# A fused attention and mixture-of-experts kernel: the row maxima travel another way, and four operands are laid out anew

## The chip, the cores and the metric

The kernel runs on one core of a Trainium2 chip. The metric is the device time of one execution, in microseconds. The core has a tensor engine (PE, with its weight loads shown apart as PEld), a vector engine (DVE), a scalar engine (ACT), a general engine (POOL) and a queue engine (SP) that here only issues transfers. Sixteen DMA engines move data between HBM and SBUF for all of them.

## The reference, cut to what matters

```python
B, H, S, D = 4, 8, 576, 64
scores = q @ k.T / 8 ; scores[above the diagonal] = -1e9
a = exp(scores - scores.max(-1)) ; a /= a.sum(-1) + 1e-9
local = a @ v
q_p = where(q > 0, q, exp(q) - 1) + 1
mem_out = (q_p @ M_prev) / (q_p . z_prev + 1e-6)
x = sigmoid(beta) * mem_out + (1 - sigmoid(beta)) * local      # [B*S=2304, 512]
# eight experts of 288 tokens each, filled greedily by the order of all logits x @ w_gate
x[mask] = maximum(x[mask] @ w1[e], 0) @ w2[e]
out = maximum(maximum(x @ w1, x @ w2), x @ w3) @ w_out
```

## The kernel before, in words

The program has three stages: attention (32 heads as 16 pairs, four pairs per batch), routing (a search for each expert's threshold), and the experts with the final block. The change touches the first stage only.

For each pair SP loads K and Q transposed (`Kr`, `Qr`, 128 partitions: the same 64 rows are loaded twice, once into each half), Q in another layout (`QN`), the memory matrix (`MZ`), and V (`V`, `VT`). The two copies serve a split of fp32 into a rounded part and a rest: `KX` holds rounded K above its rest, `QX` rounded Q twice, `KB`/`QL` the rounded K and the rest of Q.

A head's scores are computed twice. First as `s` (line 480, and 482 for the last 64 rows of both heads together), from which DVE takes minus the row maximum over 8 into a column of `nm` (line 499, one column per block of 128 rows, nine columns per pair). Then transposed as `t` (lines 598 and 599); the second product there has a 65th row of `QL` that carries the row maximum, so that ACT can take `exp` straight from PSUM (line 609) into `PT`. POOL zeroes the triangle above the diagonal (line 627), PE multiplies by V (`av`, line 642), DVE normalizes (lines 660 to 671) and adds onto `x`, into which the memory part (`mem`, line 691) was written before (line 710). Eight further columns of `x` carry the routing logits.

The row maxima stand in `nm` as columns over 128 partitions, and are wanted as one row on partition 64 of `QL`. For pairs 1 to 15 DVE copies them (`nmr`, line 533), SP writes them transposed to HBM (`nmd`, line 536, one element of 4 bytes at a time), waits, and reads them back as rows (lines 543 and 544, twice for each head). Pair 0 uses small products with an identity instead (line 559).

Beside this the stage converts the weights of the final block from 64 to 32 bits (`conv`, lines 817 to 837: a load `m2raw`, then ACT and DVE); after each batch SP stores `x` to HBM (`xd`, line 801).

The order of all this is not that of the code. `Plan.run` simulates the engines with costs and latencies that are written beside each task (`add(key, {engine: ns}, fn, deps, new, use)`), and the tasks are then emitted in the order of their simulated start; each engine and each queue runs its part strictly in that order. `new` takes a buffer out of a ring (`BUFS` has their sizes) and `use` holds it. A transfer on SP is planned as a cost on SP plus a latency (2000, or `NLAT` = 3000 for the row maxima). `fill` products without a use (line 749) keep PE occupied while the first loads come.

Of the kernel before, what the change touches and what calls it, by code (L numbers as in the profile page):

```python
# [22 lines left out]
F32 = mybir.dt.float32  # L23
# [10 lines left out]
NJ = 5  # L34
# [6 lines left out]
FILL = (48, 256)  # L41
# [13 lines left out]
BUFS = {'Kr': 2, 'Qr': 2, 'QN': 2, 'MZ': 2, 'V': 3, 'VT': 2, 'phi': 2, 'ph': 1, 'KX': 6, 'QX': 5, 'QL': 3, 'KB': 6, 'QJ': 4, 'nm': 3, 'nmr': 4, 'PT': 2, 's': 3, 't': 2, 'r5': 2, 'tmp': 3, 'rm': 2, 'x': 2, 'm2raw': 1, 'm2a': 1, 'm2b': 1}  # L55
# [172 lines left out]
def attention(g, tc, ctx, consts, beta, qT, kT, qN, v1, vT, mz, mT, wg, xd, nmd, L, m2):  # L228
# [12 lines left out]
    warm = mask[:, :256].bitcast(BF)  # L241
# [79 lines left out]
    pairs, xs, stores = [], {}, {}  # L321
    W = PRIO

    def pair(p):
# [3 lines left out]
        b_ = {n: Buf(R[n]) for n in ("Kr", "Qr", "QN", "MZ", "V", "VT", "phi", "ph")}  # L328
# [46 lines left out]
        tM = add(k0 + .2, {"SP": 300}, ldmz, new=[b_["MZ"]])  # L375
# [46 lines left out]
        def head(i):  # L422
            bh = {x: Buf(R[x]) for x in ("KX", "QX", "QL", "KB")}
            r.bh[i] = bh
            kh = n + 5 * i + W["prep"]

            def ck(e):
                r.KX[i] = tile("KX", [128, S], F32R)
                copy(e, r.KX[i], r.Kr[:, i])

            def cq(e):
                r.QX[i] = tile("QX", [128, S], F32R)
                copy(e, r.QX[i], r.Qr[:, i])
# [18 lines left out]
            t3 = add(kh + .1, sb, sk, [t1], use=[b_["Kr"], bh["KX"]])  # L452
            t4 = add(kh + .1, sb, sq, [t2], new=[bh["QL"]], use=[b_["Qr"], bh["QX"]])
# [8 lines left out]
    def maxes(r, p):  # L462
# [110 lines left out]
    def unit(r, p, i):  # L573
# [14 lines left out]
        for gi, gr in enumerate(groups):  # L588
# [22 lines left out]
            t = add(n1 + W["T"] + .1 * gi, {"PE": (430, 590, 460, 80)[gi]}, fT, r.th[i] + r.tb[i] + [tN] + (fill if h == 1 and gi == 3 else []),  # L611
# [22 lines left out]
        for j in range(NJ):  # L634
            m = rows(j)

            def fA(e, j=j, m=m):
                av = av3(AV[h % 2])
                for kb in range(j + 1):
# [6 lines left out]
                           mk[:1] + (fill if h == 1 else []) + (ex[1:2] if j else []) + (mk[1:2] if j > 1 else []) + (mk[2:] if j > 3 else []) + [r.tV],  # L646
# [3 lines left out]
    def norm(r, p, i, deps, mems):  # L650
# [25 lines left out]
        c = {"POOL": 920, "DVE": dve(360)}  # L676
        return add(n + .3, {x: c[x] for x in (W["xadd"] if p < NP - 1 else ("POOL", "DVE"))}, f4, [t] + mems, use=[bt, r.bx])

    def mem(r, p, part):
# [36 lines left out]
        return add(n + .3, {"DVE": dve(144 * k)}, f3, [t] + ([firsts[b]] if b in firsts else []),  # L716
                   new=[pend[b]] if first else [], use=[bm, br] + ([] if first else [pend[b]]))
# [3 lines left out]
    def gate(r, b, h0, h1, deps):  # L721
# [57 lines left out]
    for p in range(NP):  # L779
# [14 lines left out]
        if pp == H // 2 - 1:  # L794
            gate(r, b, H - 2 if b == B - 1 else 0, H, stores[b])

            def st(e, b=b):
                x = xs[b]
# [4 lines left out]
            add(r.n + 9 + W["gate"], {"SP": 6000}, st, stores[b], use=[r.bx])  # L803
# [652 lines left out]
def program(tc, qT, kT, qN, v1, vT, mz, mT, beta, wg, wr, w1, w2, w3, wo, out):  # L1456
    g = K()
    g.rounds, g.elist = [], []
    with tc.manual_schedule(), ExitStack() as top:
# [3 lines left out]
        nmd = dr.tile([B * H // 2, 9, 128], F32, name="nmd")  # L1463
# [5 lines left out]
        with ExitStack() as ctx:  # L1469
            attention(g, tc, ctx, consts, beta, qT, kT, qN, v1, vT, mz, mT, wg, xd, nmd, L, (w1, w2, w3, wo))  # L1470
# [8 lines left out]
def layout(i):  # L1479
    import numpy as np  # L1480
    d = {}
    for n in "qk":
        d[n + "T"] = np.ascontiguousarray(i[n].reshape(B, H // 2, 2, S, D).transpose(0, 1, 4, 2, 3))
# [12 lines left out]
    d["mz"] = mz  # L1496
# [26 lines left out]
```

## Time and profile before

| | us |
|---|---|
| median of 3 runs (1086.93 to 1127.53) | 1096.24 |
| the profiled execution's own time | 1086.32 |
| its span, first to last instruction | 1084.5 |

| engine | busy us | share of the span |
|---|---|---|
| PE | 944.3 | 87% |
| DVE | 598.3 | 55% |
| POOL | 366.2 | 34% |
| ACT | 312.3 | 29% |

The profile shows for each stretch of time how long each engine was busy, which of its two levels of clock TensorE was granted (1.00 is 2.4 GHz, 0.50 is 1.2 GHz, values between are means over a stretch), and the busy share of the 16 DMA engines with what they moved. A matmul that runs at the lower clock counts as busy for longer, so a busy PE isn't a PE at its best. A wait is put down to what ended last before it.

### The profile page before, as it was taken

How to read it: one execution, taken by the hardware profiler on the slowest of the kernel's cores; microseconds unless marked ns; L12 is line 12 of the kernel's file. 1: busy time of each engine (PE TensorE's matmuls, PEld its weight loads, DVE VectorE, ACT ScalarE, POOL GpSimd, SP SyncE). 2: the span in 40 equal slices, each digit the busy share in tenths (PEclk: the TensorE clock that was granted, in tenths of full speed). 3: DMA queues.
4: the chain of work that ended last, by engine and by line, in shares of the span. 5: the costliest groups of instructions: out<-in, count | busy, mean ns of one | idle time of the engine just before them, and what ended most of it. 6: DMA issues, size and time to landing. Idle time of an engine off the chain costs nothing.

```text
span 1084.5 us, 17202 instructions
## 1 busy us (share of the span) xinstructions
PE 944.3 (87%) x6494; PEld 869.0 (80%) x6494; DVE 598.3 (55%) x1664; ACT 312.3 (29%) x675; POOL 366.2 (34%) x344
## 2 busy tenths in 40 slices
PE   8697979987798993489799899899899799879997
PEld 6576868876687882489699799798799698779996
DVE  8556755575668548755627637538337447513221
ACT  5223321232334223041231332222331322332311
POOL 4233422342345128130630631522521523450301
PEclk8657855575859586589999899999899899899999
DMA  8777765869667711240610511602501602451100
GB/s 231 144 104 114 127 175 74 137 111 158 124 148 179 95 23 44 51 127 15 122 62 18 122 60 40 138 21 61 127 21 57 122 21 59 125 133 39 40 1 30
DMA packets 73338, 97.59 MB, mean 90 GB/s; under 512 B 46218, under 2 KB 48266, under 8 KB 73256
## 3 DMA queue, kind: packets, MB, share of 16 engines
q1 hardware_dynamic: 70280, 87.06, 40.0%
q0 software_dynamic: 2976, 9.44, 2.6%
q8 instruction: 51, 0.84, 0.3%
q14 instruction: 31, 0.25, 0.1%
HBM read 86.97 MB, written 9.52 MB: 89 GB/s over the span
## 4 chain that ended last, share of the span: by engine, by line
PE 54%; DMA 22%; DVE 12%; issue 7%; POOL 2%; ACT 1%; SPq 1%; POOLq 0%; DVEq 0%; ACTq 0%
PE av L642 7%; PE w L1270 7%; PE w L1272 7%; PE w L1271 7%; DMA m2raw<-in_m2w 6%; PE acc L1270 4%; DMA wraw<-in_wr 4%; PE acc L1272 4%; PE acc L1271 4%; DMA xg<-xd,tidx 3%; PE t L598 2%; PE s L480 2%; PE t L599 2%; DMA MZ<-in_mz 2%; DMA Qr<-in_qT 2%
## 5 line engine op out<-in xcount | busy, mean ns | idle before, releaser
L1240 POOL TENSOR_TENSOR wlo<-wraw,whi 128x1024 fp32r<-128x1024 f32 x57 | 139.3, 2448 | 308.3 <-ACT whi L1236 308.1
L1270 PE MATMUL w<-yh,mh 128*128 128x288 f32 x576 | 174.9, 304 | 8.4 <-ACT mt L1372 5.7
L1271 PE MATMUL w<-yl,mh 128*128 128x288 f32 x576 | 172.2, 299 | 0.0
L1272 PE MATMUL w<-yh,ml 128*128 128x288 f32 x576 | 171.6, 298 | 0.0
L642 PEld LDWEIGHTS av<-V,PT 128*128 128x128 f32 (+2 forms) x960 | 148.5, 230 | 14.6 <-issue 4.8
L642 PE MATMUL av<-V,PT 128*128 128x73 f32 (+2 forms) x960 | 157.4, 319 | 0.0
L1270 PEld LDWEIGHTS w<-yh,mh 128*128 128x128 f32 x576 | 110.4, 192 | 12.8 <-ACT mt L1372 5.9
L1271 PEld LDWEIGHTS w<-yl,mh 128*128 128x128 f32 x576 | 110.5, 192 | 3.5
L1272 PEld LDWEIGHTS w<-yh,ml 128*128 128x128 f32 x576 | 110.7, 192 | 0.0
L1374 DVE TENSOR_TENSOR mt<-w,mt 128x288 f32<-128x288 f32 x96 | 43.6, 454 | 106.4 <-PE w L1272 69.5
L1236 ACT CAST whi<-wraw 128x1024 fp32r<-128x1024 f32 x64 | 67.0, 1049 | 116.5 <-DMA wraw<-in_wr 109.8
L1174 DVE SCALAR_TENSOR_TENSOR hl<-w,hh 128x288 fp32r<-128x288 f32 x64 | 29.1, 457 | 129.2 <-ACT hh L1168 129.0
L627 POOL TENSOR_SCALAR_AFFINE_SELECT PT<-PT 128x256 f32<-128x256 f32 (+1 forms) x96 | 42.2, 448 | 151.8 <-ACT PT L609 146.1
L609 ACT ACTIVATE PT<-t 128x512 f32<-128x512 f32 x96 | 54.6, 595 | 135.1 <-PE av L642 76.8
L499 DVE CUSTOM_DVE_ANT_0 junk<-s,mask 128x256 bf16<-128x256 f32 (+4 forms) x145 | 72.8, 508 | 29.4 <-PE s L480 19.4
L598 PE MATMUL t<-QX,KX 128*128 128x512 f32 (+4 forms) x160 | 70.6, 448 | 20.1 <-ACT PT L609 20.1
L1270 PE MATMUL w<-xhi,whi 128*128 128x288 f32 x256 | 76.9, 300 | 0.0
L1271 PE MATMUL w<-xlo,whi 128*128 128x288 f32 x256 | 76.5, 299 | 0.0
L1272 PE MATMUL w<-xhi,wlo 128*128 128x288 f32 x256 | 76.3, 298 | 0.0
L1271 PE MATMUL acc<-hl,whi 128*128 128x288 f32 x256 | 75.6, 295 | 0.8 <-DVE hl L1174 0.8
L1270 PE MATMUL acc<-hh,whi 128*128 128x288 f32 x256 | 76.2, 298 | 0.0
L1272 PE MATMUL acc<-hh,wlo 128*128 128x288 f32 x256 | 75.4, 295 | 0.0
(234 smaller groups left out, 2022.8 us busy)
## 6 DMA issues: line engine op xcount, KB each, us to landing
wraw<-in_wr SPq DMA_DIRECT2D x64, 512.0 KB
Kr<-in_kT SPq DMA_DIRECT2D x30, 288.0 KB
Qr<-in_qT SPq DMA_DIRECT2D x30, 288.0 KB
m2raw<-in_m2w SPq DMA_DIRECT2D x12, 512.0 KB
V<-in_v SPq DMA_DIRECT2D x16, 365.0 KB
QN<-in_qN SPq DMA_DIRECT2D x16, 288.0 KB
VT<-in_vT SPq DMA_DIRECT2D x16, 288.0 KB
xd<-x SPq DMA_DIRECT2D x16, 256.0 KB
```

Source lines behind the costliest of these rows:

```text
L499: V.tensor_tensor_reduce(out=junk[ps_, :z - a], in0=o.s[ps_, :z - a], in1=mask[ps_, k:k + z - a], scale=-0.125, scalar=init, op0=OP.add, o ...
L598: nc.tensor.matmul(o.t[:kr, c:c + z - a], r.KX[i][:, ks], r.QX[i][:, a:z], start=True, stop=False)
L609: A.activation(u.PT[:kr, at0:at0 + wd], o.t[:kr, :wd], AF.Exp, scale=0.125)
L627: G.affine_select(v, v, pattern=[[1, m]] if cnt == 1 else [[0, 2], [1, m]], compare_op=OP.is_ge, fill=0.0, base=0, channel_multiplier=-1)
L642: nc.tensor.matmul(av[:m, j], u.PT[:kr, o:o + m], r.V[:kr, kb, i], start=(kb == 0), stop=(kb == j))
L1174: V.scalar_tensor_tensor(lo(), src(), 0.0, hi().bitcast(F32), op0=OP.max, op1=OP.subtract)
L1236: A.copy(x.W[fb][0], x.RAW[fb])
L1240: (V if e == "DVE" else G).tensor_sub(x.W[fb][1], x.RAW[fb], x.W[fb][0].bitcast(F32))
L1270: nc.tensor.matmul(o, wh, rh, start=start, stop=False)
L1271: nc.tensor.matmul(o, wh, rl, start=False, stop=False)
L1272: nc.tensor.matmul(o, wl, rh, start=False, stop=stop)
L1374: V.tensor_max(q.mt, o.pt[:, :T], q.mt)
```

## The change

- **Row maxima.** PE transposes `nm` with an identity into an `s` buffer in PSUM (9 rows of 128), ACT copies it to `n9` in SBUF, and three transfers from SBUF to SBUF, issued on ACT's queue, put the parts into the row of `QL`, which now is one tile per pair. `nmd`, its write and its reads are gone.
- **K and Q** are stored twice on the host side, so that one transfer over 128 partitions loads each pair's K or Q instead of two over 64. `MZ` is loaded once per batch instead of once per pair.
- **x** is split into `x2` (the 512 columns, stored to HBM in rows of 2 KB) and `x` (the logits), so two DVE steps become two instructions each.
- **Rings:** `m2raw` 2 instead of 1, `QL` 2 pairs instead of 3 heads, `KB` 5 (was 6), `QJ` 3 (was 4).
- **Fill:** 16 tasks of two products, 64 rows by 384 columns in fp32r, instead of 48 of 128 by 256 in bf16.

```diff
-FILL = (48, 256)
+FILL = (16, 384)
...
-            for a in range(2):
-                nc.sync.dma_start(t[64 * a:64 * a + 64], src[b, pp])
+            nc.sync.dma_start(t, src[b, pp])
...
-            r.MZ = tile("MZ", [128, 2 * C])
-            nc.sync.dma_start(r.MZ, mz[b, pp])
+            mzs[b].t = tile("MZ", [128, H // 2, 2 * C])
+            nc.sync.dma_start(mzs[b].t, mz[b])
...
-                u.nr = tile("nmr", [128, 9], F32R)
-                V.tensor_copy(u.nr, u.nm)
+                u.s = ps.tile([128, 512], F32, name="s", bufs=BUFS["s"])
+                nc.tensor.transpose(u.s[:9, :128], u.nm, g.ident)
             def f1(e):
-                nc.sync.dma_start(nmd[p].rearrange("c p -> p c"), u.nr.bitcast(F32))
-            t = add(n + 9 + W["N"], {"DVE": 65}, f0, ttr, new=[bf], use=[bnm])
-            t = add(n + 9 + W["N"], {"SP": 300}, f1, [t], use=[bf], lat=NLAT)
-            for i in range(2):
-                def f2(e, i=i):
-                    q = r.QL[i].bitcast(F32)[64:65]
-                    nc.sync.dma_start(q[:, :512], nmd[p:p + 1, 4 * i:4 * i + 4].rearrange("o c p -> o (c p)"))
-                    nc.sync.dma_start(q[:, 512:], nmd[p:p + 1, 8, 64 * i:64 * i + 64])
-                r.tN.append(add(n + 9 + W["N"] + .1, {"SP": 500}, f2, [t, r.tb[i][0]], use=[r.bh[i]["QL"]], lat=NLAT))
+                u.n9 = tile("n9", [9, 128], F32R)
+                copy(e, u.n9, u.s[:9, :128])
+            def f2(e):
+                q, s9 = r.QLp.bitcast(F32)[64:65], u.n9.bitcast(F32)
+                for i in range(2):
+                    nc.scalar.dma_start(q[:, i, :512].rearrange("o (j c) -> o j c", c=128), s9[4 * i:4 * i + 4])
+                nc.scalar.dma_start(q[:, :, 512:], s9[8:9].rearrange("o (i c) -> o i c", i=2))
+            t = add(n + 9 + W["N"], {"PE": 250}, f0, ttr, new=[bs], use=[bnm])
+            t = add(n + 9 + W["N"], {"ACT": act(128, True)}, f1, [t], new=[bf], use=[bs])
+            t = add(n + 9 + W["N"] + .1, {"ACT": 1200}, f2, [t, r.tb[1][0]], use=[bf, r.b["QL"]], lat=NLAT)
...
-            x = xs[b][:, :, h]
-            vg(e).tensor_add(x, x, u.tmp)
+            for x, c0, c1 in ((x2s[b].t[:, :, h], 0, 64), (xs[b][:, :, h], 64, 72)):
+                vg(e).tensor_add(x, x, u.tmp[:, :, c0:c1])
...
-                    nc.sync.dma_start(xd[r].rearrange("p (h c) -> p h c", h=H), x[:rows(j), j, :, :64])
+                    nc.sync.dma_start(xd[r], x2s[b].t[:rows(j), j].rearrange("p h c -> p (h c)"))
```

The change moves instructions on three queues. First SP, around the write of one pair's row maxima in the middle of the stage. Before:

```order
L354 DMA VT<-in_vT 128x576
L536 DMA nmd<-nmr 128x9x1
L817 DMA m2raw<-in_m2w 128x1024
L543 DMA QL<-nmd 1x512
L544 DMA QL<-nmd 1x64
L346 DMA MZ<-in_mz 128x146
L337 DMA Kr<-in_kT 64x1152 x2
L342 DMA QN<-in_qN 128x576
L543 DMA QL<-nmd 1x512
L544 DMA QL<-nmd 1x64
L337 DMA Qr<-in_qT 64x1152 x2
```

The same place of SP in the changed program:

```order
L337 DMA Qr<-in_qT 128x1152
L337 DMA Kr<-in_kT 128x1152
L350 DMA V<-in_v 128x730
L342 DMA QN<-in_qN 128x576
L337 DMA Qr<-in_qT 128x1152
L835 DMA m2raw<-in_m2w 128x1024
L354 DMA VT<-in_vT 128x576
L835 DMA m2raw<-in_m2w 128x1024
L337 DMA Kr<-in_kT 128x1152
L342 DMA QN<-in_qN 128x576
```

Only loads of whole operands are left; the write with its four reads is gone from SP, and two loads of `m2raw` can stand close together.

Second PE, in the changed program, at the end of one pair's score blocks (`qj` is the block of both heads' last rows; the row with `ident` is the new transposition):

```order
L490 MATMUL s<-KX,qj_132 128x64
L608 MATMUL t<-QX,KX 128x512
L609 MATMUL t<-QL,KB_129 128x512
L608 MATMUL t<-QX,KX 128x64
L609 MATMUL t<-QL,KB_129 128x64
L608 MATMUL t<-QX,KX 128x448
L609 MATMUL t<-QL,KB_129 128x448
L488 MATMUL s<-KX,QX 128x128
L541 MATMUL s<-ident,nm 9x128
L488 MATMUL s<-KX,QX 128x256
```

The transposition stands eight instructions behind the pair's last score product; nothing of this kind stood on PE for pairs 1 to 15 before.

Third ACT, in the changed program, where it issues the row transfers of one pair (`n` is the copy `n9`):

```order
L293 CAST n_824<-s 9x128
L293 CAST QX<-Qr 128x576
L401 ACTIVATE ph<-QN 128x576
L619 ACTIVATE PT<-av_110 64x64
L619 ACTIVATE PT<-t 128x512
L406 ACTIVATE ph<-ph 128x576
L845 ACTIVATE m2a<-m2raw 128x512
L619 ACTIVATE PT<-t 128x512
L550 DMA QL<-n_824 1x4x128 x2
L551 DMA QL<-n_824 1x2x64
L293 CAST KB_129<-Kr 64x576
```

The copy and the three transfers are new on ACT, and exponentials (`PT`) stand between and behind them.

## Rows read from the trace of the kernel before

**Rows 1.** The page: span, and each engine's busy us, share, instructions.

```profile
span 1084.5 us, 17202 instructions
PE 944.3 (87%) x6494; PEld 869.0 (80%) x6494; DVE 598.3 (55%) x1664; ACT 312.3 (29%) x675; POOL 366.2 (34%) x344
```

**Rows 2.** Stretches by stage: us, busy (instructions) by engine, clock, DMA share, GB/s.

```profile
0.00:414.00 414.00, 358.95 (x1978) 315.66 (x1978) 261.01 (x744) 136.27 (x292) 147.29 (x217) 0.69 0.69 127
414.00:452.00 38.00, 9.36 (x144) 7.66 (x145) 33.94 (x113) 6.23 (x7) 17.68 (x8) 0.53 0.22 59
452.00:1084.00 632.00, 575.99 (x4375) 545.68 (x4373) 303.32 (x809) 169.79 (x378) 201.27 (x120) 0.95 0.27 67
```

**Rows 3.** The chain that ended last: start us, us, what.

```profile
35.95 13.70 DMA Qr<-in_qT
...
177.97 13.97 DMA m2raw<-in_m2w
...
285.86 10.45 DMA MZ<-in_mz
...
378.53 10.52 DMA MZ<-in_mz
```

**Rows 4.** SP's own instructions from 285 us: start, us, engine, line, operation.

```profile
285.39 0.38 SPq L536 DMA_DIRECT2D nmd<-nmr  x1
285.86 0.68 SPq L346 DMA_DIRECT2D MZ<-in_mz  x1
...
295.05 0.25 SPq L543 DMA_DIRECT2D QL<-nmd  x1
```

**Rows 5.** The DMA view of 36 to 46 us, behind another `nmd` write.

```profile
DMA packets 875, 0.29 MB, mean 29 GB/s; under 512 B 813, under 2 KB 813, under 8 KB 875
...
q1 hardware_dynamic: 875, 0.29, 79.4%
```

**Rows 6.** The DMA view of 15 to 30 us, loads alone.

```profile
DMA packets 1638, 4.00 MB, mean 267 GB/s; under 512 B 230, under 2 KB 478, under 8 KB 1636
```

**Rows 7.** Waits, SP's queue and then PE: total us, times, longest.

```profile
SPq L543 <- DMA nmd<-nmr: 75.8, 12, 9.7
...
PE t L599 <- DMA QL<-nmd: 2.4, 1, 2.4
```

**Rows 8.** Stretches of the attention stage, columns as in Rows 2.

```profile
23.00:37.00 14.00, 11.87 (x79) 9.81 (x78) 13.53 (x40) 7.69 (x18) 8.15 (x11) 0.99 0.90 181
...
42.00:51.00 9.00, 2.57 (x10) 2.00 (x10) 1.26 (x4) 0.39 (x2) 0.00 (x0) 0.50 0.79 153
51.00:81.00 30.00, 27.56 (x112) 24.32 (x113) 15.86 (x50) 8.22 (x16) 8.31 (x12) 0.50 0.77 119
...
142.00:183.00 41.00, 41.00 (x176) 36.78 (x176) 27.14 (x78) 11.04 (x25) 14.57 (x16) 0.50 0.56 113
...
291.00:297.00 6.00, 0.00 (x0) 0.00 (x0) 0.72 (x1) 0.67 (x3) 0.17 (x1) 0.67 0.71 41
297.00:322.00 25.00, 24.91 (x104) 22.09 (x104) 16.30 (x42) 7.84 (x18) 11.53 (x14) 0.50 0.64 137
322.00:351.00 29.00, 26.25 (x194) 23.35 (x192) 23.78 (x73) 12.97 (x28) 14.51 (x48) 0.97 0.80 194
351.00:385.00 34.00, 34.00 (x146) 29.94 (x146) 17.52 (x54) 7.82 (x18) 6.73 (x9) 0.50 0.71 82
...
388.00:390.00 2.00, 0.27 (x3) 0.27 (x4) 0.93 (x3) 0.00 (x0) 0.00 (x0) 1.00 0.01 1
```

**Rows 9.** Groups of instructions in 0 to 414 us: busy us, mean ns, idle before.

```profile
L533 DVE CAST nmr<-nm 128x9 fp32r<-128x9 f32 x15 | 7.3, 487 | 0.0
L660 DVE TENSOR_SCALAR r<-av,c 128x5 f32<-128x5 f32 x32 | 7.1, 221 | 15.2 <-PE av L642 15.1
L292 ACT COPY V<-mem 128x80 f32<-128x80 f32 x15 | 3.5, 231 | 16.4 <-PE mem L383 8.8 <-DMA V<-in_v 7.7
L559 PE MATMUL t<-identr,nmr 128*1 128x128 f32 x8 | 1.2, 283 | 0.0
```

More of the change, by code (lines that the diff above doesn't have):

```diff
@@ L54 @@
 FK = {"m2": -600, "m2b": -40, "ml": ("POOL",), "load": -30, "wsplit": -12, "wlo": ("POOL",), "gather": -60, "xt": -50, "h1": 0, "y": 3, "o": 6, "store": 57.5, "idx": -30}
-BUFS = {'Kr': 2, 'Qr': 2, 'QN': 2, 'MZ': 2, 'V': 3, 'VT': 2, 'phi': 2, 'ph': 1, 'KX': 6, 'QX': 5, 'QL': 3, 'KB': 6, 'QJ': 4, 'nm': 3, 'nmr': 4, 'PT': 2, 's': 3, 't': 2, 'r5': 2, 'tmp': 3, 'rm': 2, 'x': 2, 'm2raw': 1, 'm2a': 1, 'm2b': 1}
+BUFS = {'Kr': 2, 'Qr': 2, 'QN': 2, 'MZ': 2, 'V': 3, 'VT': 2, 'phi': 2, 'ph': 1, 'KX': 6, 'QX': 5, 'QL': 2, 'KB': 5, 'QJ': 3, 'nm': 3, 'nmr': 1, 'n9': 1, 'PT': 2, 's': 3, 't': 2, 'r5': 2, 'tmp': 3, 'rm': 2, 'x': 2, 'm2raw': 2, 'm2a': 1, 'm2b': 1, 'x2': 2}
 OFFK = (0, 576, 1024, 1344, 1536)
@@ L225, with attention @@
        "SP": dict.fromkeys(("PE", "DVE", "ACT", "POOL", "SP"), 2000)}
-def attention(g, tc, ctx, consts, beta, qT, kT, qN, v1, vT, mz, mT, wg, xd, nmd, L, m2):
+def attention(g, tc, ctx, consts, beta, qT, kT, qN, v1, vT, mz, mT, wg, xd, L, m2):
     nc = tc.nc
@@ L240, in attention @@
     nc.vector.memset(mask, 0.0)
-    warm = mask[:, :256].bitcast(BF)
+    warm = cs.tile([128, 512], F32R, name="warm")
+    nc.vector.tensor_copy(warm, mask[:, :512])
     nc.gpsimd.affine_select(mask[:, 512:640], mask[:, 512:640], pattern=[[-1, 128]], compare_op=OP.is_ge,
@@ L319, in attention @@
         pass
-    pairs, xs, stores = [], {}, {}
+    pairs, xs, stores, mzs, x2s = [], {}, {}, {}, {}
     W = PRIO
@@ L327, in pair @@
         r.n = 10 * p
-        b_ = {n: Buf(R[n]) for n in ("Kr", "Qr", "QN", "MZ", "V", "VT", "phi", "ph")}
+        b_ = {n: Buf(R[n]) for n in ("Kr", "Qr", "QN", "MZ", "V", "VT", "phi", "ph", "QL")}
         r.b = b_
@@ L364, in f @@
                         setattr(r, name, tile(name, [128, 2, S]))
-                    for a in range(2):
-                        nc.sync.dma_start(getattr(r, name)[64 * a:64 * a + 64, i], src[b, pp, :, i])
+                    nc.sync.dma_start(getattr(r, name)[:, i], src[b, pp, :, i])
                 return f
@@ L374, in pair @@
         tN = add(k0 + .1, {"SP": 900}, ldqn, new=[b_["QN"]])
-        tM = add(k0 + .2, {"SP": 300}, ldmz, new=[b_["MZ"]])
+        if pp == 0:
+            mzs[b] = K()
+            mzs[b].b = b_["MZ"]
+            tM = add(k0 + .2, {"SP": 800}, ldmz, new=[b_["MZ"]])
+        b_["MZ"] = mzs[b].b
         tV = add(k0 + .3, {"SP": 1000}, ldv, new=[b_["V"]])
@@ L415, in scale @@
         def scale(e):
-            copy(e, r.MZ.rearrange("p (i c) -> p i c", i=2)[:, :, 64:72], MG[:, p])
-        r.tmz = add(kp + .1, {"POOL": 110, "ACT": 75, "DVE": 70}, scale, [tM, tmg[b]], use=[b_["MZ"]])
+            copy(e, mzs[b].t.rearrange("p q (i c) -> p (q i) c", i=2)[:, :, 64:72], MG[:, p:p + 4].rearrange("p q i e -> p (q i) e"))
+        if pp == 0:
+            mzs[b].ts = add(kp + .1, {"POOL": 240, "ACT": 120, "DVE": 120}, scale, [tM, tmg[b]], use=[b_["MZ"]])
+        r.tmz = mzs[b].ts
         r.KX, r.QX, r.QL, r.KB, r.th = {}, {}, {}, {}, {}
@@ L422, in head @@
         def head(i):
-            bh = {x: Buf(R[x]) for x in ("KX", "QX", "QL", "KB")}
+            bh = {x: Buf(R[x]) for x in ("KX", "QX", "KB")}
+            bh["QL"] = b_["QL"]
             r.bh[i] = bh
@@ L438, in sq @@
             def sq(e):
-                r.QL[i] = tile("QL", [65, S], F32R)
+                if not i:
+                    r.QLp = tile("QL", [65, 2, S], F32R)
+                r.QL[i] = r.QLp[:, i]
                 vg(e).tensor_sub(r.QL[i][:64], r.Qr[:64, i], r.QX[i][:64].bitcast(F32))
@@ L452, in head @@
             t3 = add(kh + .1, sb, sk, [t1], use=[b_["Kr"], bh["KX"]])
-            t4 = add(kh + .1, sb, sq, [t2], new=[bh["QL"]], use=[b_["Qr"], bh["QX"]])
+            t4 = add(kh + .1, sb, sq, [t2] + ([r.tb[0][0]] if i else []), new=[] if i else [bh["QL"]], use=[b_["Qr"], bh["QX"]] + ([bh["QL"]] if i else []))
             t5 = add(kh + .2, cp, cb, [tK[i]] + tkb[2 * p + i:2 * p + i + 1], new=[bh["KB"]], use=[b_["Kr"]])
@@ L609, in fE @@
                 A.activation(u.PT[:kr, at0:at0 + wd], o.t[:kr, :wd], AF.Exp, scale=0.125)
-            t = add(n1 + W["T"] + .1 * gi, {"PE": (430, 590, 460, 80)[gi]}, fT, r.th[i] + r.tb[i] + [tN] + (fill if h == 1 and gi == 3 else []),
+            t = add(n1 + W["T"] + .1 * gi, {"PE": (430, 590, 460, 80)[gi]}, fT, r.th[i] + r.tb[i] + [tN] + (fill if p == 0 and gi == 3 else []),
                     new=[bt], use=list(bh.values()))
@@ L645, in unit @@
             out.append(add(n1 + W["A"] + .1 * j, {"PE": (168, 382, 596, 810, 628)[j]}, fA,
-                           mk[:1] + (fill if h == 1 else []) + (ex[1:2] if j else []) + (mk[1:2] if j > 1 else []) + (mk[2:] if j > 3 else []) + [r.tV],
+                           mk[:1] + (fill if p == 0 else []) + (ex[1:2] if j else []) + (mk[1:2] if j > 1 else []) + (mk[2:] if j > 3 else []) + [r.tV],
                            use=[bP, r.b["V"], r.bav[i]]))
@@ L675, in norm @@
         t = add(n + .2, {"DVE": dve(360)}, f3, [t], new=[bt], use=[br, r.bav[i]])
-        c = {"POOL": 920, "DVE": dve(360)}
-        return add(n + .3, {x: c[x] for x in (W["xadd"] if p < NP - 1 else ("POOL", "DVE"))}, f4, [t] + mems, use=[bt, r.bx])
+        c = {"POOL": 1020, "DVE": dve(320) + 90}
+        return add(n + .3, {x: c[x] for x in (W["xadd"] if p < NP - 1 else ("POOL", "DVE"))}, f4, [t] + mems, use=[bt, r.bx, r.bx2])
     def mem(r, p, part):
@@ L690, in f0 @@
                 m = rows(j)
-                nc.tensor.matmul(MEM[:m, 2 * C * jj:2 * C * jj + 2 * C], r.phi[:, 128 * j:128 * j + m], r.MZ, start=True,
+                nc.tensor.matmul(MEM[:m, 2 * C * jj:2 * C * jj + 2 * C], r.phi[:, 128 * j:128 * j + m], mzs[b].t[:, pp], start=True,
                                  stop=True)
@@ L704, in mem @@
             pend[b] = Buf(R["x"])
+            x2s[b] = K()
+            x2s[b].b = Buf(R["x2"])
         r.bx = pend[b]
+        r.bx2 = x2s[b].b
         def f3(e):
             if first:
-                xs[b] = tile("x", [128, NJ, H, 72])
-            V.tensor_mul(xs[b][:, js[0]:js[-1] + 1, 2 * pp:2 * pp + 2], mv[:, :k, :, :72],
-                         u.rm[:, :k, :, None].to_broadcast([128, k, 2, 72]))
+                xs[b] = tile("x", [128, NJ, H, 8])
+                x2s[b].t = tile("x2", [128, NJ, H, 64])
+            for dst, c0, c1 in ((x2s[b].t, 0, 64), (xs[b], 64, 72)):
+                V.tensor_mul(dst[:, js[0]:js[-1] + 1, 2 * pp:2 * pp + 2], mv[:, :k, :, c0:c1],
+                             u.rm[:, :k, :, None].to_broadcast([128, k, 2, c1 - c0]))
         t = add(n, {"PE": 251 * k}, f0, [r.tphi, r.tmz], new=[bm], use=[r.b["phi"], r.b["MZ"]])
@@ L715, in mem @@
         t = add(n + .2, {"DVE": 80}, f2, [t], use=[br])
-        return add(n + .3, {"DVE": dve(144 * k)}, f3, [t] + ([firsts[b]] if b in firsts else []),
-                   new=[pend[b]] if first else [], use=[bm, br] + ([] if first else [pend[b]]))
+        return add(n + .3, {"DVE": dve(144 * k) + 70}, f3, [t] + ([firsts[b]] if b in firsts else []),
+                   new=[pend[b], x2s[b].b] if first else [], use=[bm, br] + ([] if first else [pend[b]]))
     pend, firsts = {}, {}
@@ L748, in attention, with fw @@
     for k in range(FILL[0]):
-        fill.append(add(1e5 + k, {"PE": FILL[1] * 0.4167}, lambda e: nc.tensor.matmul(
-            AV[1][:, :FILL[1]], warm[:, :128], warm[:, :FILL[1]], start=True, stop=True)))
+        def fw(e, k=k):
+            for i in range(2):
+                q = slice(64 * i, 64 * i + 64)
+                nc.tensor.matmul(AV[i][:, :FILL[1]], warm[q, :128], warm[q, :FILL[1]], start=True, stop=True)
+        fill.append(add(1e5 + k, {"PE": 2 * FILL[1] * 0.4167}, fw))
     tmg = []
@@ L1469, in program @@
         with ExitStack() as ctx:
-            attention(g, tc, ctx, consts, beta, qT, kT, qN, v1, vT, mz, mT, wg, xd, nmd, L, (w1, w2, w3, wo))
+            attention(g, tc, ctx, consts, beta, qT, kT, qN, v1, vT, mz, mT, wg, xd, L, (w1, w2, w3, wo))
         rt = top.enter_context(tc.tile_pool(name="route", bufs=1, reuse_waits="tile"))
@@ L1482, in layout @@
     for n in "qk":
[L1483 removed]
+        t = i[n].reshape(B, H // 2, 2, S, D).transpose(0, 1, 4, 2, 3)
+        d[n + "T"] = np.concatenate([t, t], axis=2)
     d["qN"] = np.ascontiguousarray(i["q"].transpose(0, 1, 3, 2)).reshape(B, H // 2, 128, S)
```

13 lines of the change are left out of this document (6 added, 7 removed).

## The prediction

> **What bounds the kernel now.** I read the page first: PE is busy for 944.3 of 1084.5 us, so the first question is what its busy time is made of [rows 1]. The stretches by stage answer it: in attention, 0 to 414 us, PE is busy for 358.95 us at a mean clock of 0.69, while behind 452 us it is busy for 575.99 of 632 us at 0.95 [rows 2]. The change touches the first stage alone. The two later stages keep their instructions, so I carry their 670 us over unchanged. What the first stage can lose is 414 − 358.95 = 55 us in which PE idles, and the time that it works at the lower clock.
>
> Next the chain. In attention eight transfers of 10 to 14 us lie on it, four of them shown, and even an `MZ` load of 128 x 146 floats (75 KB) takes 10.45 us [rows 3]. SP's queue says why: each of the eight was issued behind a write of `nmd`, as at 285.39 us, and SP could send the read back only at 295.05 [rows 4]. While such a write runs, the 16 DMA engines are 79.4% busy and move 29 GB/s, 813 of 875 packets being under 512 B; loads alone move 267 GB/s [rows 5, 6]. The write has 1152 elements of 4 bytes. Whatever was issued after it stands behind it, and SP itself waits 75.8 us in total for these writes [rows 7].
>
> Then the windows, which show what PE makes of that. Each of the eight transfers ends in a hole, the first at 42 to 51 us (2.57 busy of 9), the last at 388 to 390; eight holes, 38.7 us of idle PE. Behind a hole the clock is at 0.50 and stays there: seven stretches, from 51 to 81 us to 297 to 322 us, hold 161.5 us of busy PE at 0.50 [rows 8]. In 142 to 183 us PE is busy for all of 41.00 us at 0.50, 233 ns for one matmul, against 26.25 us for 194, or 135 ns, in 322 to 351 us at 0.97 [rows 8]. So the price of the writes is the hole and, larger, the clock after it.
>
> **The change part by part.** All against the profiled execution (1086.3 us), which is 9.9 us under the median of 1096.24.
>
> 1. *The 15 writes and 60 reads through HBM go.* The eight holes go: −38.7 us. If nothing else lowered the clock, the 161.5 us would run at the other rate, 161.5 x (1 − 135/233) = −67.9 us. SP is free of its 75.8 us of waits, so loads start when their buffer comes free.
>
> 2. *What is late next: DVE, and a clock that still drops.* Not every drop begins with a transfer. Before 37 us DVE was busy for 13.53 of 14 us, PE for 11.87, and the clock fell; at 351 us it fell again and stayed down for 34 us with PE never idle [rows 8]. I count four such drops in 146 us at full clock (twelve stretches), one per 36 us, followed by 7, 5, 4 and 34 us at 0.50, on the mean 12.5; the seven after holes last 23.1. I take 15, nearer to the four, because their cause is the one that is left. A cycle is then 36 us with PE busy for 0.905 of it at 135 ns (241 matmuls) and 15 us at 233 ns (64). The stage has 1978 matmuls and gets 15 more: 1993/305 x 51 = 333 us. Bounds: no drops at all gives 1993 x 0.135/0.905 = 297 us; drops as now, with only the holes gone, 414 − 38.7 = 375 us.
>
> 3. *The transpositions.* 15 on PE, nearest row 283 ns for a 128 x 128 product: 4.2 us, of which 2 are in the 1993 already, so +2 us [rows 9]. PE now waits there for DVE's last minimum. No row has that wait. Its bounds are 0 (the three `s` buffers tie PE to the same minima anyway) and 15 x 2.43 = 36 us, by the one wait of PE for a row of maxima [rows 7]; I take 3 us, because eight instructions stand between the last score product and the transposition.
>
> 4. *ACT.* 15 copies at the 231 ns of a similar PSUM copy, and 45 issues at the 0.25 us that SP needs for one: 14.7 us [rows 4, 9]. ACT is busy for 136.27 of 414 us [rows 2], so its idle time hides it: 0. Without that cover, 14.7. Exponentials queue behind the issues, and PE waits for those; the delay is 0.75 us per pair at most.
>
> 5. *DVE.* 15 casts go (−7.3 us), 64 second halves come, each under the 221 ns of the smallest shape near it (+14) [rows 9]. Half of the +7 on the path: +3 us.
>
> 6. *Relaid K, Q, MZ and x, the second `m2raw`, the fill.* The bytes of K and Q are the same; the loads were not slow when alone [rows 6]. The 16 `MZ` loads become 4. The rings `KB` and `QJ` get smaller, which costs when PE is behind DVE, not while it waits for data. The second `m2raw` takes away waits that the writes caused, already counted. The fill covers the same 12,288 columns. 0 for all, between −5 and +5.
>
> Sum: attention 333 + 2 + 3 + 3 = 341 us instead of 414, that is 1086.3 − 73 = **1013 us**. As a check, DVE would be busy for 268 of 341 us, 79%, less than the 82% of 322 to 351 us [rows 8].
>
> **The rivals.**
>
> *The clock never drops.* Attention takes 297 us, DVE 90% busy, and the kernel 1086.3 − 117 = 969 us. For it: full clock lasted 29 us with PE at 0.905. Against it: the drops without a hole, 351 us among them [rows 8]. The Trainium skill, "TensorE: Matmul & The Clock Gate", section "Why this matters for your kernels", says that continuous work takes TensorE to its full rate and idle gaps take it back; by that the kernel without holes would come out at this rival's time. The 41.00 busy us at 0.50 [rows 8] disagree with the first half of the rule. This rival gets 0.10.
>
> *Only the holes close.* The work between them stays at the lower clock as often as now: 375 + 8 = 383 us, 1055 us, up to 1068 when the wait at the transpositions is nearer to its upper bound. For it: 351 to 385 us. Against: of the 211 busy us at 0.50 in these eleven stretches 161.5 came behind a hole. 0.14.
>
> *The row arrives late.* The transfers of 2 KB wait behind the loads in the DMA engines, now that SP issues loads unhindered. At 94 us PE stood for 2.43 us for such a row [rows 7]; 15 of these are 36 us, with a drop of the clock after some of them about 36 us more: 1013 + 72 = 1085 us, no change. Against: it happened once in 30 reads although the same engines served them. The Trainium skill, "DMA: Bandwidth & Descriptors", section "Issuing engines are not separate DMA queues", says that transfers from all queues end up on the same 16 engines and interleave; by that ACT's queue gives the row no path of its own, but the row no longer stands behind all that SP has queued. 0.05.
>
> *Slower: PE settles at the lower clock.* With PE always at work and always at 0.50, as from 142 to 183 us, 1993 matmuls at 233 ns are 464 us, and the kernel takes 1086.3 + 58 = 1144 us. It decides against the change as soon as some 300 us of the stage's busy time are at 0.50 (now the 211 of the eleven stretches and a few in between): then 300 + (1993 − 300/0.233) x 0.135 / 0.905 = 405 us plus 8 reach 414. Denser work could do this only if idle time helped the clock, which no row shows. 0.06.
>
> **How the numbers follow.** My forecast gets 0.65 and the four rivals 0.10, 0.14, 0.05 and 0.06. The predicted time is the forecast's 1013. Cycles with cold stretches of 8 to 30 us instead of 15 give 319 to 355 us, 999 to 1035, and terms 3 to 6 at their bounds 30 more upwards. The range from 965 to 1068 takes in the first two rivals and leaves out the last two and some of the edges. Two per cent, about what a measurement of this kernel can tell from no change, is 1065 us and below. Faster: 0.65, 0.10 and nearly half of the second rival, 0.81. Same: the rest of that and the third, 0.12. Slower: 0.07.
>
> **What would show it.** Right: no stretch with the DMA engines above 70% busy under 60 GB/s; SP's waits on transfers nearly gone; holes of PE over 3 us at most twice before the end of attention; mean clock of the stage above 0.8; the stage ending near 341 us and the rest 670 us long. Wrong: holes that end with a transfer of `QL` or with DVE at the transposition (term 3), a mean clock still near 0.69 (term 2), or a later stage that is longer.

## The result

The changed kernel takes 1012.76 us in the median of four runs (1007.76 to 1022.49), the kernel before 1093.46 us in four (1086.93 to 1127.53): a ratio of 0.9291, 95% interval 0.9187 to 0.9395, some 7% faster. The forecast was 1013 us in a range of 965 to 1068. Ratios here and below leave out disturbed runs, so they are not the quotients of the medians. The profiled execution took 1015.55 us.

### The profile page after: what moved, and what is told of

Its sections match the earlier page's. It is cut to its first block, busy times and chain, and to the rows that moved or that the text cites. A ratio compares the mean times of both kernels' runs of the same rounds, so it can differ in the third digit from the quotient of the medians.

```text
span 1013.8 us, 17122 instructions
## 1 busy us (share of the span) xinstructions
PE 914.2 (90%) x6493; PEld 842.0 (83%) x6493; DVE 592.6 (58%) x1704; ACT 317.0 (31%) x687; POOL 363.2 (36%) x342
## 2 busy tenths in 40 slices
DMA packets 37598, 97.52 MB, mean 96 GB/s; under 512 B 9620, under 2 KB 9740, under 8 KB 37516
## 4 chain that ended last, share of the span: by engine, by line
PE 63%; DVE 12%; DMA 10%; issue 8%; POOL 4%; ACT 2%; ACTq 0%; SPq 0%; POOLq 0%; DVEq 0%
PE av L652 10%; PE w L1288 7%; PE w L1289 7%; PE w L1290 7%; PE acc L1288 4%; PE acc L1290 4%; PE acc L1289 4%; DMA xg<-xd,tidx 4%; DMA wraw<-in_wr 4%; PE s L488 3%; PE t L608 3%; PE t L609 2%; PE mem L701 2%; PE mem L386 2%; POOL xg L1218 2%
## 5 line engine op out<-in xcount | busy, mean ns | idle before, releaser
L652 PEld LDWEIGHTS av<-V,PT 128*128 128x128 f32 (+2 forms) x960 | 136.2, 214 | 13.4 <-issue 4.9
L652 PE MATMUL av<-V,PT 128*128 128x73 f32 (+2 forms) x960 | 145.9, 303 | 0.3 <-ACT PT L619 0.3
L507 DVE CUSTOM_DVE_ANT_0 junk<-s,mask 128x512 bf16<-128x512 f32 (+4 forms) x145 | 72.9, 507 | 36.7 <-PE s L488 31.0
L488 PE MATMUL s<-KX,QX 128*128 128x128 f32 (+3 forms) x128 | 61.3, 490 | 5.6 <-DVE nm L507 3.1
```

Of the source, the lines that this page charges most:

```text
L488: nc.tensor.matmul(o.s[:, :z - a], r.QX[i][:, 128 * j:128 * j + 128], r.KX[i][:, a:z], start=True, stop=True)
L507: V.tensor_tensor_reduce(out=junk[ps_, :z - a], in0=o.s[ps_, :z - a], in1=mask[ps_, k:k + z - a], scale=-0.125, scalar=init, op0=OP.add, o ...
L652: nc.tensor.matmul(av[:m, j], u.PT[:kr, o:o + m], r.V[:kr, kb, i], start=(kb == 0), stop=(kb == j))
```

## The profile after

The page of the changed kernel, answering to [rows 1]: the span, the engines, the row of slices of TensorE's clock, the DMA packets and two of the DMA queues (packets, MB, share of 16 engines).

```profile
span 1013.8 us, 17122 instructions
...
PE 914.2 (90%) x6493; PEld 842.0 (83%) x6493; DVE 592.6 (58%) x1704; ACT 317.0 (31%) x687; POOL 363.2 (36%) x342
...
PEclk9556885597799857998999999998999999989999
...
DMA packets 37598, 97.52 MB, mean 96 GB/s; under 512 B 9620, under 2 KB 9740, under 8 KB 37516
...
q1 hardware_dynamic: 34240, 86.92, 30.1%
...
q10 hardware_dynamic: 300, 0.07, 0.0%
```

PE lost 30 us of busy time, and in the first third four fifths of its idle time. The new queue q10 is the one on which ScalarE sends the rows: 300 packets, no share of the DMA engines that shows. In the slices of PEclk one sees that the low clock is still there.

The stages of the changed kernel, with the columns of [rows 2]: length, busy time and instructions of PE, PEld, DVE, ACT and POOL, granted clock, DMA share, GB/s.

```profile
0.00:344.40 344.40, 332.50 (x1977) 292.92 (x1977) 254.26 (x781) 140.84 (x303) 144.67 (x215) 0.77 0.46 153
344.40:381.00 36.60, 7.38 (x123) 5.83 (x123) 32.68 (x109) 5.78 (x6) 17.92 (x8) 0.52 0.13 43
381.00:1013.80 632.80, 574.33 (x4393) 543.26 (x4393) 305.67 (x816) 170.41 (x378) 200.58 (x120) 0.96 0.28 68
```

Against [rows 2] attention went from 414 to 344.4 us, the other two stages from 670 to 669.4. In attention PE's idle time fell from 55.0 to 11.9 us (344.40 − 332.50), by 43 us, and its busy time from 358.95 to 332.50, by 26 us for nearly the same work (1977 products where it was 1978), which goes with the clock: 0.77 where it was 0.69. The two make the 70 us.

The stretches of the attention stage in the changed kernel, cut where the clock changes, as [rows 8] was:

```profile
0.00:26.00 26.00, 22.52 (x121) 16.50 (x121) 15.90 (x55) 10.92 (x26) 6.04 (x17) 1.00 0.80 297
26.00:29.00 3.00, 1.37 (x11) 1.11 (x10) 2.59 (x9) 2.02 (x6) 1.85 (x2) 0.94 0.50 146
29.00:93.00 64.00, 64.00 (x279) 57.36 (x279) 36.87 (x118) 22.27 (x51) 23.31 (x29) 0.50 0.38 127
93.00:117.00 24.00, 23.62 (x176) 20.75 (x174) 23.49 (x74) 12.24 (x28) 12.11 (x15) 0.99 0.57 184
117.00:134.00 17.00, 16.41 (x74) 14.50 (x74) 11.73 (x36) 6.70 (x14) 6.78 (x8) 0.51 0.54 174
134.00:155.00 21.00, 19.72 (x145) 17.27 (x145) 20.52 (x63) 10.70 (x23) 11.42 (x16) 0.99 0.70 236
155.00:202.00 47.00, 47.00 (x204) 41.91 (x204) 29.66 (x83) 15.90 (x33) 15.15 (x18) 0.50 0.44 140
202.00:227.00 25.00, 24.01 (x180) 21.55 (x180) 23.94 (x72) 14.45 (x31) 12.65 (x16) 0.98 0.65 218
227.00:236.00 9.00, 9.00 (x39) 8.43 (x40) 8.95 (x22) 2.30 (x5) 4.25 (x4) 0.50 0.61 196
236.00:250.00 14.00, 11.62 (x86) 9.84 (x85) 12.74 (x33) 8.03 (x17) 9.08 (x9) 0.97 0.60 211
250.00:267.00 17.00, 17.00 (x74) 15.12 (x73) 11.95 (x36) 5.36 (x12) 8.29 (x11) 0.52 0.40 128
267.00:344.40 77.40, 76.23 (x606) 68.58 (x604) 55.92 (x192) 29.95 (x63) 33.76 (x75) 1.00 0.22 66
```

Read two columns against each other. In the full-clock stretches from 93 to 250 us DVE is busy nearly throughout (23.49 of 24 us, 23.94 of 25) and PE stands now and then; at 0.50 PE is busy nearly all the time and DVE, but for 227 to 236 us, has room. Behind the start no hole like the 2.57 busy of 9 us in [rows 8] is left; in steps of 3 us the largest idle time is 1.67 us, in 246 to 249 us. What falls in its place is the clock, each time behind a stretch in which DVE was the busier engine or nearly so; in the last 77 us DVE is busy for 55.92, and the clock stays up. That DVE brings the drops is read from these rows and not shown.

The chain of waits of the changed kernel (start, length, what) has three transfers in attention, the longest of 4.89 us; the chain before had ten of 10 to 14 us, four of them in [rows 3]:

```profile
93.23 2.82 DMA QN<-in_qN
...
100.28 3.16 DMA Qr<-in_qT
...
208.76 4.89 DMA Qr<-in_qT
```

## The experiments

Eleven kernels were run in three sessions: the first four together, the next three together on another chip, the last four together, each set beside runs of the kernel before. The changed kernel's own ratio is 0.9291 in the result and 0.9037 in the last session, so differences of a per cent or two are read only between kernels of one session.

**The row path alone, in the kernel before.** Only the transposition, the copy and ScalarE's transfers are put in (with `QL` in one tile, which they need); K, Q, MZ, x and `m2raw` stay.

```diff
-                u.nr = tile("nmr", [128, 9], F32R)
-                V.tensor_copy(u.nr, u.nm)
...
-                nc.sync.dma_start(nmd[p].rearrange("c p -> p c"), u.nr.bitcast(F32))
+                u.s = ps.tile([128, 512], F32, name="s", bufs=BUFS["s"])
+                nc.tensor.transpose(u.s[:9, :128], u.nm, g.ident)
...
+                    nc.scalar.dma_start(q[:, i, :512].rearrange("o (j c) -> o j c", c=128), s9[4 * i:4 * i + 4])
```

> The kernel before with the row maxima alone moved (transposition on PE, copy and three transfers on ACT, QL as a pair tile); K, Q, MZ, x, the fill and m2raw stay as they were. Theory W (the 4-byte writes hold the DMA engines, loads behind them come late, and TensorE's clock falls after each hole): most of the gain, 1030 us (1010 to 1055), attention some 350 to 365 us long, no 1 us stretch with DMA busy and under 60 GB/s for 8 us on end. Rival L (the relaid operands, the second m2raw or the fill carry the gain): 1075 to 1095 us.

Measured: 1014.9 us (1005.02 to 1017.83), ratio 0.9249 (0.915 to 0.9348). Its attention stage:

```profile
0.00:340.80 340.80, 319.26 (x1992) 278.51 (x1993) 262.94 (x733) 134.36 (x299) 147.15 (x218) 0.80 0.58 154
```

The whole gain is in the row path, and the stage is shorter than the 350 to 365 us expected. The kernel has 28,789 packets under 512 B against 9,620 in the changed kernel, and no cost of them shows: the relaid operands save packets that were in nobody's way.

**Everything but the row path.** The changed kernel, with the maxima written to HBM and read back by SP, as before.

```diff
+                nc.sync.dma_start(nmd[p].rearrange("c p -> p c"), u.nr.bitcast(F32))
...
+                    nc.sync.dma_start(q[:, :512], nmd[p:p + 1, 4 * i:4 * i + 4].rearrange("o c p -> o (c p)"))
```

> The changed kernel with the maxima written to HBM and read back as before; all other parts of the change stay. Theory W: 1060 to 1095 us, holes of 4 to 9 us behind the writes as before. Rival L: 1015 to 1030 us.

Measured: 1109.29 us (1087.46 to 1123.61), ratio 0.9971 (0.9878 to 1.0063): no gain left; the median is above the 1095 us expected, in a session where the kernel before took 1105.94. The stage in the profiled execution, and then SP's longest wait in it (total us, times, longest), that for the write:

```profile
0.00:413.20 413.20, 370.14 (x1961) 327.42 (x1962) 251.21 (x794) 138.95 (x291) 140.39 (x214) 0.69 0.61 127
```

```profile
SPq L551 <- DMA nmd<-nmr: 99.7, 14, 9.1
```

**The write alone, which nobody reads.** The changed kernel, order of the other engines unchanged, with SP also writing the maxima of 15 pairs to HBM, 1152 elements of 4 bytes each time.

```diff
+                nc.sync.dma_start(nmd[p].rearrange("c p -> p c"), u.nm)
```

> The changed kernel, same order on PE, DVE, ACT and POOL, with one more transfer on SP's queue for each of the 15 pairs: the maxima are also written to HBM element by element (1152 packets of 4 bytes), and nobody reads them. Theory W: the occupied DMA engines alone bring the holes back, 1045 to 1085 us. Rival Q (what delayed the loads was SP standing in order for the write before it could issue the reads and what followed): 1010 to 1020 us, since nobody waits for this write.

**The same bytes in rows.** As the last, but each of 128 partitions writes its 36 bytes in one piece.

```diff
-                nc.sync.dma_start(nmd[p].rearrange("c p -> p c"), u.nm)
+                nc.sync.dma_start(nmd[p].rearrange("c p -> (c p)").rearrange("(p c) -> p c", c=9), u.nm)
```

> As the kernel with the extra element-wise write, but the same 4.6 KB go as 128 rows of 36 bytes. It has the same entry in SP's queue and the same wait of SP for DVE's last minimum. Theory W: 1012 to 1022 us, as the changed kernel. If SP's wait for DVE or the additional transfer itself is what costs: the time of the element-wise one.

Measured: 1062.12 us (1051.31 to 1064.03), ratio 0.9672 (0.9571 to 0.9772), for the elements; 1010.47 us (997.82 to 1020.71), ratio 0.9231 (0.9103 to 0.9358), for the rows. Both have the same instruction on SP, issued at 42.2 us and followed by the same loads. The DMA view of 42 to 52 us in the kernel that writes elements:

```profile
DMA packets 1221, 0.25 MB, mean 25 GB/s; under 512 B 1168, under 2 KB 1168, under 8 KB 1221
...
q1 hardware_dynamic: 1221, 0.25, 81.3%
```

and in the one that writes rows:

```profile
DMA packets 1011, 2.65 MB, mean 265 GB/s; under 512 B 247, under 2 KB 255, under 8 KB 1009
...
q1 hardware_dynamic: 989, 2.62, 78.2%
```

The engines are nearly as busy in both; the one moves a tenth of the bytes of the other. The busy share alone does not tell the two apart, the GB/s beside it do. PE's side of it in the kernel that writes elements, the hole behind that write and then the whole stage:

```profile
48.00:51.00 3.00, 1.69 (x12) 1.26 (x10) 3.00 (x9) 0.38 (x2) 1.43 (x1) 0.97 0.92 28
51.00:54.00 3.00, 0.00 (x0) 0.00 (x0) 1.37 (x4) 0.00 (x0) 0.00 (x0) 0.50 0.52 77
54.00:60.00 6.00, 2.65 (x8) 2.27 (x9) 0.00 (x0) 1.63 (x4) 1.66 (x2) 0.50 1.00 356
...
0.00:388.90 388.90, 339.06 (x1976) 297.27 (x1977) 252.42 (x781) 140.34 (x303) 144.45 (x215) 0.77 0.58 136
```

The stage in the kernel that writes rows, whose profiled execution was its fastest:

```profile
0.00:325.60 325.60, 305.45 (x1976) 266.33 (x1977) 256.18 (x781) 140.37 (x303) 148.38 (x215) 0.88 0.50 162
```

With the elements PE idles for 49.8 us of the stage, with the rows for 20.2, in the changed kernel for 11.9. By the ratios of the kernels timed together the elements give back (0.9672 − 0.9231) x 1100 = 48 us of the gain, by the intervals give or take 18; the remaining 0.030 or 33 us, give or take 15, up to the kernel that lacks the row path comes when the row itself goes through HBM and SP stands for 99.7 us until the writes have landed. In the profiled executions those last 24 us (413.2 − 388.9) are not idle time of PE (43.1 against 49.8 us) but busy time at a clock of 0.69 in place of 0.77. Why the clock is lower there was not separated further.

The kernel that writes rows also shows how far one order of work varies: PE, DVE, ACT and POOL have the changed kernel's order in it, and their stage takes 325.6 us at a clock of 0.88 where that took 344.4 at 0.77.

**Wide products against the low clock.** Of 128x512 bf16 products two, then four, are put at the head of each head's transposed scores; the next product overwrites their result. The planned cost of that block on PE is raised with them, so the order of work on all engines shifts too. The edit with four:

```diff
+                if gi == 0:
+                    wb = warm.bitcast(BF)
+                    for _ in range(4):
+                        nc.tensor.matmul(o.t, wb[:, :128], wb[:, :512], start=True, stop=True)
...
-            t = add(n1 + W["T"] + .1 * gi, {"PE": (430, 590, 460, 80)[gi]}, fT, r.th[i] + r.tb[i] + [tN] + (fill if p == 0 and gi == 3 else []),
+            t = add(n1 + W["T"] + .1 * gi, {"PE": (1290, 590, 460, 80)[gi]}, fT, r.th[i] + r.tb[i] + [tN] + (fill if p == 0 and gi == 3 else []),
```

> The changed kernel with two extra products of 128 rows by 512 columns in bf16 (zeros, overwritten afterwards) ahead of each of the 32 heads' transposed scores. They add 64 products, about 14 us at full clock and 27 us at the lower one. Theory A (in the long stretches at 0.50 the clock stays down because the products there are thin, 73 to 146 columns behind a weight load; wide ones bring it back): the stretches at 0.50 shrink from some 155 us to under 80 us and the time falls to 985 to 1005 us. Rival I (only idle time and chance decide, or the products are just more work): the same 150 us at 0.50 and 1025 to 1045 us.

> The same with four such products per head, 128 in all, about 28 us at full clock. Theory A: the clock stays up nearly throughout attention (mean above 0.93), 990 to 1010 us. Rival I: 1035 to 1070 us.

Measured: with two 1005.37 us (985.23 to 1026.35), ratio 0.907 (0.8941 to 0.9199), too wide to decide; with four 1001.01 us (996.13 to 1006.02), ratio 0.9164 (0.9097 to 0.9231). The stage with four, and two stretches of it:

```profile
0.00:324.70 324.70, 308.29 (x2104) 257.31 (x2105) 255.01 (x788) 139.94 (x295) 146.60 (x216) 0.94 0.49 162
51.00:84.00 33.00, 31.69 (x235) 26.47 (x235) 30.92 (x89) 18.49 (x40) 19.18 (x22) 1.00 0.63 200
96.00:132.00 36.00, 33.16 (x242) 27.74 (x241) 35.42 (x100) 18.62 (x38) 17.25 (x19) 1.00 0.74 242
```

PE does 128 products more in 20 us less than in the changed kernel's profiled execution. It idles for longer (16.4 us against 11.9), so they don't fill gaps; the clock is 0.94 where it was 0.77. But the kernel that writes rows, without any added product, has a stage as short (325.6 us at 0.88), so one profiled execution settles no gain in time. In 96 to 132 us DVE is busy for 35.42 of 36, as if it were now the bound.

**Additions on POOL too.** The planner was allowed to put the 64 additions into `x` on POOL as well as on DVE.

```diff
-'xadd': ['DVE']
+'xadd': ['DVE', 'POOL']
```

> The changed kernel with the additions onto x2 and x allowed on POOL as well as on DVE (only DVE before the last pair in the changed kernel). If DVE is what is late next once the writes are gone (step 2 of the prediction), fewer holes of PE come with DVE busy, so fewer drops of the clock: 985 to 1005 us. If the drops do not depend on DVE's load, or POOL becomes late with the masks: 1010 to 1030 us.

Measured: 998.14 us (990.75 to 1024.83), ratio 0.9097 (0.9033 to 0.9162). The experiment failed: in its trace all 64 additions are on DVE, and only the order of other work had shifted. Its time lies where a relieved DVE was expected, and DVE was not relieved. It is also as short as that of four products in the same session (1001.01 us), so a shift of the order alone cannot be told there from the products; what the shift is worth is open, because the changed kernel was not run beside it.

**The changed kernel again, beside four and eight products and a version with both remedies.** Four products were timed a second time; eight differ in the count; the last has four, and the additions forced to POOL (`'xadd': ['POOL']`).

> The changed kernel itself, timed beside the next three on one chip, so that these can be compared with it. Its four runs so far lie at 1007.76 to 1022.49 us. Expected: 1012 us, range 1000 to 1022, mean granted clock 0.87 to 0.90.

> The changed kernel with four 128x512 products more at the head of each transposed score group (128 in all, their result is overwritten), again, beside the changed kernel. Theory A (the low clock is settled by what TensorE did just before, and wide products keep it up): 1000 us, range 994 to 1008, 5 to 18 us below the changed kernel, mean clock 0.92 or more. Theory I (the clock has its own rhythm and the first run was luck): added products cost at least their own 128 x 0.22 = 28 us, 1035 to 1045.

> Eight such products per head, 256 in all. Theory A: the clock has nearly nothing left to gain over four (in the profile with four, about 40 of 325 us of the attention were at 0.50), so the 128 further products cost their own 128 x 0.22 = 28 us less at most 12 us: 1012 to 1030. If the clock were worth more than that, 1000 or less. Theory I: 1060 or more.

> The kernel with four products per head, and the 64 additions of the attention's result to x (128x320 at a median of 0.48 us and 128x40) on POOL in place of DVE. With four products DVE is busy nearly all of the full-clock stretches. Theory D (DVE is the bound once the clock stays high): DVE loses 64 additions of 0.18 to 0.5 us, some 21 us; the attention 5 to 20 us shorter: 980 to 996. Theory P (TensorE is still the bound, DVE only beside it): 996 to 1006. A third way: POOL, with about 1 us for such an addition, comes late and holds the buffers: 1005 to 1020.

Measured, in a session where the kernel before took 1137.81 us: the changed kernel 1020.91 us (1008.55 to 1045.43), ratio 0.9037 (0.8953 to 0.9121); four products 1007.93 us (1006.02 to 1017.63), 0.8985 (0.8923 to 0.9048); eight 1024.76 us (1019.55 to 1031.23), 0.913 (0.907 to 0.9191); four and POOL 999.53 us (996.86 to 1007.04), 0.8908 (0.8851 to 0.8964). The attention stages, in this order, one kernel each:

```profile
0.00:338.90 338.90, 326.42 (x1976) 287.39 (x1977) 253.64 (x781) 140.45 (x303) 146.47 (x215) 0.81 0.47 155
```

```profile
0.00:326.70 326.70, 309.60 (x2104) 259.63 (x2105) 256.05 (x788) 139.68 (x295) 146.56 (x216) 0.91 0.49 161
```

```profile
0.00:336.30 336.30, 323.41 (x2233) 259.31 (x2233) 259.92 (x796) 135.65 (x293) 146.22 (x210) 0.98 0.48 157
```

```profile
0.00:316.10 316.10, 303.89 (x2105) 254.07 (x2105) 240.92 (x736) 137.24 (x290) 184.12 (x273) 0.96 0.50 166
```

Eight products are slower than four, with ranges apart: at eight the clock is 0.98, and the further 128 cost more than they bring. The added products of the first kernel with four, busy us and then the mean ns of one:

```profile
L607 PE MATMUL t<-warm 128*128 128x512 bf16 x128 | 36.3, 409 | 0.0
```

One lasts 0.41 us, but the next starts before it ends, and PE is busy with the 128 for 36.3 us, 0.28 each; I had used 0.22. Four are ahead of the changed kernel by 0.6%, 6 us, in the ratios, and the intervals overlap: a gain in time is not settled. A higher clock is: 0.917 to 0.932 over the whole kernel in the twelve runs with four, 0.872 to 0.897 in the changed kernel's eight up to 1022.49 us, and at most 0.913 in the kernel that writes rows. With the additions of all but the last pair on POOL (DVE busy for 240.92 us in place of 256) the stage is 10.6 us shorter still. The time is the one expected if PE is still the bound (996 to 1006), not the one expected if DVE is (980 to 996); its interval overlaps that of four products, and the order shifts here as well, so what DVE's relief is worth is not shown. Against the changed kernel beside it this version is 1.4% lower in the ratio, and every run of it lies under every run of that one. It has the lowest ratio of its session.

## Why the prediction was right, and where it was not

*Step 1, the writes* was right. Idle time of PE fell by 43 us, against 38.7 for the eight holes, and the kernel that brings back only the 4-byte writes brings back holes (49.8 us idle). The chain before held ten transfers of 10 to 14 us and not eight; the two others, `Kr` at 17.50 us and `V` at 60.85, end in none of the eight holes. The working also put two costs into one: SP's wait and the way through HBM got no share beside the DMA engines, and 33 us of some 81 come back only with them; the two were not separated.

*Step 2, what is late next* was right in kind and in sum, and wrong in both its sizes. Its cycle implies 313 us of busy PE and 28 of idle; measured are 332.5 and 11.9. One drop per 36 us of full clock was good: five drops in 190 us (344.4 less the cold 154). But the five cold stretches of 64, 17, 47, 9 and 17 us last 31 us on the mean, not 15: of the four in the kernel before, one had lasted 34 us at 351 us [rows 8], and that is near what came, not the 4 to 7 of the others. The opposite error: I had carried over 0.905 and 135 ns for the full clock from one stretch of the kernel before. PE is busy for 0.94 of the four such stretches from 93 to 250 us (0.83 to 0.98 of each), at those 135 ns a product, and for 76.23 of the last 77.40 us, at 126 ns. So the mean clock came to 0.77 and not above 0.8, the one sign that failed. The agreement of 344 with 341 us is partly luck; in another execution the same stage takes 338.9 us, and 325.6 in the kernel that writes rows beside it.

*Step 3, the transpositions* was right: 15 of them, and PE stood before four of them for 2.0 us in all; the wait that this makes is ACT's, below.

*Step 4, ACT*: hidden, as said, but dearer. The instructions of ScalarE and its queue in the changed kernel, the three transfers of one pair (start, length):

```profile
284.65 1.22 ACTq L550 DMA_DIRECT2D QL<-n  x2
285.89 0.60 ACTq L551 DMA_DIRECT2D QL<-n  x1
```

and its longest wait at the transposition (total us, times, longest), with the transposition and the copy as groups:

```profile
ACT n L293 <- PE s L541: 19.6, 8, 5.3
```

```profile
L541 PE MATMUL s<-ident,nm 128*9 128x128 f32 x15 | 4.7, 312 | 0.7 <-DVE nm L507 0.7
...
L293 ACT CAST n<-s 9x128 fp32r<-9x128 f32 x15 | 3.8, 250 | 19.7 <-PE s L541 19.6
```

An issue takes 0.60 us on ScalarE, not the 0.25 that I took from SP [rows 4]: 45 are 28 us, with the copies 32 instead of 14.7, and 19.6 us of waiting were not priced at all. ACT is busy for 140.84 of 344.4 us, the issues not counted, and no product waits for a late row.

*Step 5, DVE*: the sign was wrong. DVE is busy for 254.26 us, 7 less and not 7 more. Splitting the additions onto `x` and the memory part did cost what was forecast, +16 us of instruction time against +14 (the 128x40 additions take 0.46 us each and not under 0.22, but the first halves got shorter). In the new order, though, the planner has more casts on ACT: of the 32 casts of K to `KX`, DVE keeps 13 where it had 21, ACT does 19 where it did 11. That is 7 us less on DVE; the rest of the difference was not followed. DVE's group in the changed kernel (busy us, mean ns, idle before):

```profile
L293 DVE CAST KX<-Kr 128x576 fp32r<-128x576 f32 x13 | 9.4, 724 | 0.0
```

*Step 6, the relaid operands, the second `m2raw`, the fill*: nothing, as forecast, and shown from both sides (0.9249 with the row path alone, 0.9971 without it).

The rivals. *The clock never drops*: five drops, so no; its 297 us is not far, though, from the 316.1 us of the last version, which hold 35 us of added products. *Only the holes close*: the clock rose too. *The row arrives late*: in the changed kernel it doesn't; in the kernel that writes elements PE waits 7.7 us once for a row that ScalarE sent behind such a write. That agrees with the Trainium skill, "DMA: Bandwidth & Descriptors", section "Issuing engines are not separate DMA queues": transfers from all issuing engines run on the same 16 engines. *PE settles at the lower clock*: 154 us of the stage are cold, half of the 300 at which that decides. Yet 64.00 busy us of 64 at 0.50 disagree, as 41.00 did [rows 8], with the Trainium skill, "TensorE: Matmul & The Clock Gate", section "Why this matters for your kernels", that continuous work takes TensorE to its full rate.

## What to carry to other kernels

Where the DMA engines are some 80% busy and move 25 to 29 GB/s, as behind the element writes here, look for a transfer of single elements, and price it by all that is queued behind it. Turn the data on chip. The same bytes written in one piece for each partition cost nothing that could be measured either, but nobody read them here: the turning would be left to the read, and that was not tried. When a stall goes, ask which engine is late next and what the clock does behind it, and bound that by cold stretches at least as long as the longest in the trace (41 us here, and one of 64 came), not by a mean of four. And compare an edit that shifts the order of work with several executions: the same order took 325.6 to 344.4 us for this stage.

## What the runs showed of the hardware that was not expected

- 1152 elements of 4 bytes, 15 times, cost some 48 us against 128 rows of 36 bytes, 15 times (ratio 0.9672 against 0.9231); of the rows no cost shows (0.9249 with the row path alone, in the same session).
- With 128 added 512-column products the clock was higher (0.81 to 0.91 in the attention stages of one session, 338.9 and 326.7 us), though PE's idle time grew from 12.5 to 17.1 us. Whether the products or the order that shifted with them do it was not separated.
- An issue of the row transfers takes 0.60 us on ScalarE's queue, that of a small transfer between SBUF and HBM 0.25 to 0.38 on SP's [rows 4]. Queue and kind of transfer were not separated.
- In eight runs of one and the same kernel the mean clock lay between 0.872 and 0.897 and the time between 1022.49 and 1007.76 us, the longest at the lowest clock.
